# Chunked attention and a routed expert layer: tokens stored by expert together with their data, instead of lists and row gathers

## The chip, the core and the metric

The kernel runs on one NeuronCore of a Trainium2 chip. A core has a matrix engine (TensorE, "PE" in the profile, with its weight loads as "PEld"), a vector engine (VectorE, "DVE"), a scalar engine (ScalarE, "ACT"), a general engine (GpSimd, "POOL"), and a queue engine (SyncE, "SP") that issues DMA transfers. ScalarE and GpSimd issue transfers too. All transfers of the core run on the same 16 DMA engines. The engines run side by side and wait for one another on semaphores.

The metric is the device time of one execution in microseconds (us), as the median of several runs.

## What is computed

Attention within chunks of 64 positions, then a router that sends each token to one of eight experts, each a two-layer network. Cut to what matters:

```python
# q, k, v: (8, 8, 576, 64) = batch, heads, positions, head size
scores = q_c @ k_c.T / sqrt(64)          # within chunks of 64 positions
attn = softmax(scores)
out = attn @ v_c
# bridge: (B, H, S, D) -> x of (4608 tokens, 512)

xn = x / (norm(x) + 1e-6)
en = expert_emb / (norm(expert_emb) + 1e-6)
logits = xn @ en.T / tau                 # 8 experts
expert_idx = argmax(logits, axis=1)
gate_w = softmax(logits)[own expert]
for e in range(8):
    mask = expert_idx == e
    h = maximum(x[mask] @ w1[e], 0)      # w1[e]: 512 x 1024
    out[mask] = gate_w[mask] * (h @ w2[e])   # w2[e]: 1024 x 512
```

All of it is in float32. Which token goes to which expert is only known when the kernel has computed the logits, so the second half works on addresses from data.

## The kernel before

The **attention stage** goes through 36 tiles of 128 tokens (`NT = 36`), as a software pipeline: in pass `t` tile `t+7` is loaded, `t+3` is transposed, scores of `t+2` and values of `t` are computed, then the logits of `t-2`. Every four tiles the router picks the experts and counts each token's place within its expert.

```python
def values(t):
    ...                                   # pv = attention weights @ v
    x = wk.tile([P, NPAIR, 2, Dh], FP32, tag="x", name="x", bufs=3)
    nc.vector.tensor_tensor(x..., pv[...], rs..., ALU.mult)
    nc.gpsimd.dma_start(out=x_rows[P * t : P * t + P, :], in_=x)
```

Each token also has a record of 16 words, `rec`: its 8 logits, the four numbers of its quarter rows (4 x token + 0..3), its own number (`TOK`) and the sum of its squares (`SQ`). A record is scattered to the token's place in the list `spots`, where every expert has room for all tokens:

```python
def put(n):
    for at, m in to_put[:n]:              # at: places of 128 tokens, m: their records
        nc.gpsimd.indirect_dma_start(out=spots, out_offset=...(ap=at, axis=0), in_=m, ...)

def clear_spots():                        # all places get a number that is no token's
    nc.sync.dma_start(out=spots..., in_=empty...)   # 2.3 MB, in pass 0
```

The **expert stage** works on groups of 64 places of one expert, two groups (`s` = 0 and 1, one for each half of the partitions) in a step `j`. For these inputs there are 73 groups, so 37 steps: 3 early ones (`NE`), whose groups are the first three of the first and of the last expert, and 34 more. 36 steps are laid out in the code; the rest are under `tc.If`. A step's tokens are read from the list, and their x gathered in four quarters of 128 columns:

```python
def load_quarters(j, eng=nc.sync, e_t=ENG.SP):
    for s in range(2):
        row = number(src_row[...], SPARE, e_t)      # a register from SBUF
        group[s, j] = spots[ds(row, G), :]
        for b in range(G // Q):                     # 2 loads of 32 x 4 numbers
            eng.dma_start(out=quarter[:, j, c : c + 1], in_=group[s, j][...])

def load_tokens(j, eng=nc.sync):                    # the records, 64 B a token
    for s in range(2):
        eng.dma_start(out=spot[G * s : G * s + G, j], in_=group.pop((s, j)))

def gather_x(j, n=N, parts=range(P // Q)):
    xin[j] = xin_sb[j % XBUF]                       # XBUF = 3
    for c in parts:                                 # 4 gathers of 128 rows of 512 B
        nc.gpsimd.indirect_dma_start(
            out=xin[j][:, c * P : c * P + P], out_offset=None,
            in_=x_rows[0:n].rearrange("n (r d) -> (n r) d", d=P),
            in_offset=...(ap=quarter[:, j, c : c + 1], axis=0), ...)
```

Then `turn_xb(j)` transposes x in blocks of 32 x 32 on VectorE, `hidden` multiplies by w1 in four parts (`h_ps`, line 247), and `result` by w2 (`y_ps`, line 267):

```python
def hidden(j, turn=None):
    for s in range(2):
        for b in range(G // Q):
            hidden_part(j, s, b, ps_h, "h")
        if s == 0 and turn is not None:
            turn_xb(turn)
            if turn + XBUF < NJ:
                gather_x(turn + XBUF)

def result(j, ps_y):
    ...                                             # matmuls, y scaled by the gate
    nc.gpsimd.indirect_dma_start(out=out, out_offset=...(spot[:, j, TOK]), in_=y, ...)
```

In the steady part TensorE does `hidden(j+1)`, then `result(j)`, and so on. `gates(j)` computes the gate from the record on VectorE and ScalarE. The weights of the next groups (2 MB for each of w1 and w2 and each half) are loaded by SP into the second buffers, where the expert changes.

The **seam** is between the two: the last tiles' places, the table of groups (`groups`, `places`) and the first lists, while TensorE works on the three early steps. Their tokens are found early, from the first 20 tiles:

```python
    if t == early_t - 2: count_early()              # early_t = 27
    if t == early_t:     load_early()               # the records of the early groups
    ...                                             # quarter numbers by a small matmul
    if t > early_t + 3:  gather_x(i // 4, PLACED, [i % 4])   # one or two in a pass
    ...
groups(); places(0, 2); gather_x(2, PLACED); turn_xb(1); hidden_part(0, 1, 1, ps_t, "tr")
places(2, NST)
...
load_spot(NE); gather_x(NE); load_spot(NE + 1); gather_x(NE + 1); ...
```

The start loads, in this order: the experts' vectors, q and k of tiles 0 and 1, v of batch 0, q and k of tiles 2 and 3, v of batch 1. q goes through GpSimd, k and v through SP.

Of the kernel before, what the change touches and what calls it, by code (L numbers as in the profile page):

```python
# [18 lines left out]
P = 128  # L19
# [6 lines left out]
def kernel(  # L26
# [41 lines left out]
    x_rows = nc.dram_tensor("x_rows", (N, D), FP32, kind="Internal").ap()  # L68

# [3 lines left out]
    TOK, SQ = E + 4, E + 5  # L73
    SPARE = E * N
    FOLD = SPARE // P + 1
    spots = nc.dram_tensor("spots", (P * FOLD, MW), FP32, kind="Internal").ap()

# [11 lines left out]
    quarter = keep.tile([P, NJ, P // Q], I32, name="quarter")  # L89
# [38 lines left out]
    group = {}  # L128

    def load_quarters(j, eng=nc.sync, e_t=ENG.SP):  # L130
        for s in range(2):
            row = number(src_row[G * s : G * s + 1, j - NE : j - NE + 1], SPARE, e_t)
            group[s, j] = spots[ds(row, G), :]
            for b in range(G // Q):
                c = s * (G // Q) + b
                eng.dma_start(
                    out=quarter[:, j, c : c + 1],
                    in_=group[s, j][Q * b : Q * b + Q, E : E + 4]
                    .bitcast(I32)
                    .rearrange("i r -> r i")  # L140
                    .unsqueeze(2),
                )

    def load_tokens(j, eng=nc.sync):
        for s in range(2):
            eng.dma_start(out=spot[G * s : G * s + G, j], in_=group.pop((s, j)))

    def load_spot(j):
        load_quarters(j)
        load_tokens(j)  # L150

    def gather_x(j, n=N, parts=range(P // Q)):


        xin[j] = xin_sb[j % XBUF]
        for c in parts:
            nc.gpsimd.indirect_dma_start(  # L157
                out=xin[j][:, c * P : c * P + P],
                out_offset=None,
                in_=x_rows[0:n].rearrange("n (r d) -> (n r) d", d=P),  # L160
                in_offset=bass.IndirectOffsetOnAxis(ap=quarter[:, j, c : c + 1], axis=0),
                bounds_check=n * (D // P) - 1,
                oob_is_err=False,
            )

    def load_early():

        for s in range(2):
            r0 = (0, E - 1)[s] * N
            nc.scalar.dma_start(  # L170
                out=spot[G * s : G * s + G, 0:NE],
                in_=spots[r0 : r0 + G * NE, :].rearrange("(j p) m -> p j m", p=G),
            )
# [120 lines left out]
    with (  # L294
# [20 lines left out]
        FB = 17  # L315
        empty = one.tile([P, FB, MW], FP32, name="empty")
        io_i = one.tile([P, NST], I32, name="io_i")
        io = one.tile([P, NST], FP32, name="io")
        rec = one.tile([P, NT, MW], FP32, name="rec")
# [11 lines left out]
        eqb = one.tile([P, NT, E], BF16, name="eqb")  # L331
        e_of = one.tile([P, NST], FP32, name="e_of")


        same = one.tile([P, P // Q, Q], FP32, name="same")
        in_q = one.tile([P, P // Q], FP32, name="in_q")
        no_q = one.tile([P, P // Q], FP32, name="no_q")
        q_of = one.tile([P, 1], FP32, name="q_of")
# [3 lines left out]
        tok4 = one.tile([P, NE, P // Q], FP32, name="tok4")  # L342

        def constants():
            nc.gpsimd.iota(
                rec[:, :, E : E + 4].bitcast(I32),
                pattern=[[4 * P, NT], [1, 4]],
                base=0,
                channel_multiplier=4,
            )  # L350
            nc.gpsimd.iota(
                rec[:, :, E + 4 : MW].bitcast(I32),
                pattern=[[P, NT], [0, MW - E - 4]],
                base=0,
                channel_multiplier=1,
            )
# [4 lines left out]
            nc.gpsimd.memset(empty.bitcast(I32), NO_ROW)  # L361
            nc.gpsimd.memset(ones, 1.0)
            nc.gpsimd.memset(before, 0.0)
            nc.gpsimd.memset(jump[:, 1], 1.0)
            nc.gpsimd.memset(nb[:, 0:1], float((SPARE + N) // G))
# [3 lines left out]
            nc.gpsimd.tensor_scalar(e_base, io[:, 0:E], float(N), None, ALU.mult)  # L369
            nc.gpsimd.tensor_scalar(second, at, float(G), None, ALU.is_ge)  # L370
            nc.gpsimd.tensor_scalar(step, second, -2.0, 1.0, ALU.mult, ALU.add)
# [3 lines left out]
            nc.gpsimd.tensor_tensor(ends_e, ends_e, full, ALU.add)  # L375

        def late_constants():
            blocks = ident.rearrange("p (c i) -> p c i", i=Q)
            nc.vector.tensor_reduce(in_q, blocks, axis=AX.X, op=ALU.add)
            for c in range(P // Q):  # L380
                nc.vector.tensor_reduce(
                    same[:, c], blocks.rearrange("p c i -> p i c"), axis=AX.X, op=ALU.add
                )
            nc.vector.tensor_tensor(no_q, in_q, io[:, 0 : P // Q], ALU.mult)
            nc.vector.tensor_reduce(q_of, no_q, axis=AX.X, op=ALU.add)
            for x in xin_sb:
                nc.vector.memset(x, 0.0)

        def clear_spots():
            nc.sync.dma_start(  # L390
                out=spots.rearrange("(p a b) m -> p a (b m)", p=P, b=FB),
                in_=empty.rearrange("p b m -> p (b m)")
                .unsqueeze(1)
                .to_broadcast([P, FOLD // FB, FB * MW]),
            )
# [19 lines left out]
        def load_v(b):  # L415

            t = v_sb[b % 2]
            for h in range(H):
                r0 = CH * (h % 2)
                nc.sync.dma_start(  # L420
                    out=t[r0 : r0 + CH, h // 2, :, 0:Dh],
                    in_=v[b, h].rearrange("(c k) d -> k c d", k=CH),
                )
            v_t[b] = t
# [53 lines left out]
        def values(t):  # L478
# [3 lines left out]
            for i in range(NPAIR):  # L482
# [14 lines left out]
            x = wk.tile([P, NPAIR, 2, Dh], FP32, tag="x", name="x", bufs=3)  # L497
            nc.vector.tensor_tensor(  # L498
                x.rearrange("p i r d -> p r i d"),
# [4 lines left out]
            x = x.rearrange("p i r d -> p (i r d)")  # L504
            nc.gpsimd.dma_start(out=x_rows[P * t : P * t + P, :], in_=x)  # L505
            st[t] = {"x": x}

        def turn_x(t):
            d = st[t]
            ps = ps_t.tile([P, KD, P], FP32, tag="tr", name="tr")  # L510
            for c in range(KD):
# [6 lines left out]
                junk, d["x"], AF.Square, accum_out=rec[:, t, SQ : SQ + 1]  # L518
# [13 lines left out]
        def pick(b):  # L532
# [3 lines left out]
            lg = rec[:, t : t + n, 0:E]  # L536
# [12 lines left out]
        def place(b):  # L549
# [33 lines left out]
            if t + n < NT:  # L583
                with nc.allow_low_precision("whole numbers up to 36"):
                    if n == 1:
                        nc.vector.tensor_tensor(before, before, eqb[:, t], ALU.add)
                    else:
                        nc.vector.tensor_reduce(
                            before,
                            eqb[:, 0 : t + n].rearrange("p s e -> p e s"),  # L590
                            axis=AX.X,
                            op=ALU.add,
                        )
            to_put.extend((dest[:, i : i + 1], rec[:, t + i]) for i in range(n))

        to_put = []

        def early_rows(part):


            ps = rt_ps[:, 3, 1:4].rearrange("p a b -> p (a b)")[:, 0 : NE * (P // Q)]
            ps = ps.rearrange("p (j c) -> p j c", j=NE)
            if part == 0:
                nc.vector.scalar_tensor_tensor(
                    out=tok4,
                    in0=spot[:, 0:NE, TOK : TOK + 1].bitcast(I32).to_broadcast([P, NE, P // Q]),
                    scalar=float(P // Q),
                    in1=in_q.unsqueeze(1).to_broadcast([P, NE, P // Q]),
                    op0=ALU.mult,
                    op1=ALU.mult,  # L610
                )
            elif part == 1:
                nc.tensor.matmul(
                    ps, lhsT=same.rearrange("p c i -> p (c i)"), rhs=tok4, start=True, stop=True
                )
            else:
                nc.vector.tensor_scalar(quarter[:, 0:NE], ps, q_of, None, ALU.add)

        def count_early():
# [3 lines left out]
            nc.vector.tensor_scalar(done, cnt, float(G), None, ALU.is_ge)  # L623
            for i in range(1, NE):
                nc.vector.tensor_scalar(full, cnt, float(G * (i + 1)), None, ALU.is_ge)
                nc.vector.tensor_tensor(done, done, full, ALU.add)
            nc.vector.tensor_tensor(done, done, ends_e, ALU.mult)

        def put(n):

            for at, m in to_put[:n]:
# [9 lines left out]
                tc.add_to_no_dep_group("spots", ins.ins)  # L641
            del to_put[:n]

# [5 lines left out]
        def groups():  # L649
# [21 lines left out]
                jump[:, 0], nb[:, 0:E], -float(G), float(N), ALU.mult, ALU.add  # L671
# [65 lines left out]
        nc.sync.dma_start(out=emb, in_=moe_expert_emb)  # L737
        nc.sync.dma_start(out=tau_sb, in_=moe_tau.unsqueeze(0).to_broadcast([E, 1]))
        for t in range(2):
            load_qk(t)  # L740
# [3 lines left out]
        load_v(0)  # L744
        for t in range(2, 4):
            load_qk(t)
        load_v(1)
        constants()

# [175 lines left out]
```

## Time and profile before

| | |
|---|---|
| median of 3 runs | 796.28 us (792.1 to 801.57) |
| span of the profiled run | 796.7 us |
| mean granted TensorE clock | 0.963 |
| moved by the core's DMA engines | 133.14 MB, mean 167 GB/s |
| packets, and those under 512 B | 147384, 109076 |
| GpSimd's indirect DMAs | 160 gathers of x, 37 scatters of y, 36 scatters of records |

Attention lasts until some 215 us of the span, the expert steps from then on. "Busy" of TensorE is modelled and overlaps, so its rate is read from how many records fall into a stretch, not from its busy time. In the chain of waits each line is a start, a duration and what took that time. Two weight-and-matmul records stand for one float32 matmul of the code.

### The profile page before, as it was taken

What the parts mean: (1) busy time and instruction counts of PE and PEld (TensorE: products, weight loads), DVE (VectorE), ACT (ScalarE), POOL (GpSimd) and SP (SyncE); (2) the same over time, 40 slices, a digit from 0 to 9 for tenths busy, and PEclk for the clock granted to TensorE, in tenths of its full rate; (3) what the DMA queues carried; (4) which work ended last, traced back from release to release, by engine and by line L of the source; (5) the groups of instructions that cost most, each with busy time, mean ns of one, the idle gap of its engine ahead of it and who ended that gap; (6) DMA issues with size and microseconds to landing.
All of it is one profiled execution on the core that took longest, in us unless ns stands there. A gap on an engine that the chain in (4) does not pass through costs nothing.

```text
span 796.7 us, 25216 instructions
## 1 busy us (share of the span) xinstructions
PE 719.9 (90%) x10328; PEld 504.4 (63%) x10328; DVE 269.1 (34%) x755; ACT 288.5 (36%) x518; POOL 295.9 (37%) x337
## 2 busy tenths in 40 slices
PE   2699999988668899999999999999999999999994
PEld 2588888877335566767567566666667565665651
DVE  1387777765352122222212212213212222122100
ACT  3265666544113224242332332423333333324102
POOL 5135555534553333333423433332434334234130
PEclk9999999997758999999999999999999999999998
DMA  9999999998113561114676515789651444412240
GB/s 164 228 275 235 246 238 229 228 301 316 43 25 114 188 225 36 35 36 148 218 274 207 191 34 196 255 299 341 232 172 36 141 147 147 134 36 80 83 141 10
DMA packets 147384, 133.14 MB, mean 167 GB/s; under 512 B 109076, under 2 KB 111828, under 8 KB 147264
## 3 DMA queue, kind: packets, MB, share of 16 engines
q1 hardware_dynamic: 131792, 92.99, 42.2%
q0 software_dynamic: 15056, 38.46, 16.1%
q8 instruction: 83, 1.36, 0.7%
q14 instruction: 37, 0.30, 0.1%
q10 hardware_dynamic: 416, 0.02, 0.0%
HBM read 349.63 MB, written 21.80 MB: 466 GB/s over the span
## 4 chain that ended last, share of the span: by engine, by line
PE 80%; issue 7%; DMA 4%; DVE 3%; SPq 2%; another core or an unknown queue 2%; POOL 1%; ACT 0%; POOLq 0%; DVEq 0%
PE h_ps L247 32%; PE y_ps L267 32%; PE rt_ps L524 3%; PE tr L431 3%; DMA kx<-in_k_dram 2%; PE sc L447 2%; PE pv L487 2%; PE tr L473 2%; PE tr L512 2%; SPq L420 2%; DMA w<-in_moe_w_dram 1%; DVE x L498 1%; POOL qx L408 0%; DMA qx<-in_q_dram 0%
## 5 line engine op out<-in xcount | busy, mean ns | idle before, releaser
L247 PE MATMUL h_ps<-w,xbT 128*32 128x256 f32 x4736 | 304.7, 387 | 12.2 <-issue 9.2
L267 PE MATMUL y_ps<-w,hT 128*32 128x512 f32 x2368 | 298.8, 593 | 10.9 <-issue 9.5
L247 PEld LDWEIGHTS h_ps<-w,xbT 128*32 128x32 f32 x4736 | 235.2, 111 | 72.0 <-issue 40.2
L157 POOL DMA_INDIRECT xin<-x_rows,quarter x160 | 161.3, 1008 | 184.7 <-DVE xbT L208 130.8
L267 PEld LDWEIGHTS y_ps<-w,hT 128*32 128x32 f32 x2368 | 127.4, 110 | 145.9 <-issue 133.3
L257 DVE STREAM_TRANSPOSE hT<-h 128x512 f32<-128x512 f32 x74 | 52.6, 711 | 337.7 <-ACT h L256 311.6
L256 ACT ACTIVATE h<-h_ps 128x512 f32<-128x512 f32 x74 | 44.2, 597 | 262.3 <-PE h_ps L247 202.2
L276 POOL DMA_INDIRECT out_dram<-y,spot x37 | 37.6, 1016 | 187.5 <-ACT y L275 173.9
L275 ACT ACTIVATE y<-y_ps,gate 128x512 f32<-128x512 f32 x37 | 25.4, 687 | 94.7 <-PE y_ps L267 89.9
L228 ACT ACT_TABLE_LOAD x37 | 47.5, 1283 | 24.7 <-DVE sh L227 8.8
L505 POOL DMA_DIRECT2D x_rows<-x x36 | 20.6, 573 | 78.1 <-DVE x L498 52.5
L223 ACT ACT_TABLE_LOAD x37 | 47.5, 1283 | 2.9 <-DMA w<-in_moe_w_dram 2.2
L514 ACT COPY xT<-tr 128x512 f32<-128x512 f32 x36 | 21.1, 587 | 71.8 <-PE tr L512 54.2
L524 PE MATMUL rt_ps<-enT,xT 128*128 128x8 f32 x288 | 37.2, 255 | 10.9 <-DVE rec L540 8.7
L524 PEld LDWEIGHTS rt_ps<-enT,xT 128*128 128x128 f32 x288 | 37.5, 202 | 12.9 <-DVE rec L540 4.8
L431 PE MATMUL tr<-ident,kx 128*128 128x128 f32 x144 | 24.7, 298 | 22.0 <-DMA kx<-in_k_dram 21.3
L632 POOL DMA_INDIRECT spots<-rec,dest x36 | 36.4, 1012 | 19.1 <-issue 14.0
L208 DVE STREAM_TRANSPOSE xbT<-xin 128x256 f32<-128x256 f32 x74 | 43.4, 624 | 0.1
L408 POOL DMA_DIRECT2D qx<-in_q_dram x40 | 35.2, 884 | 21.6 <-PE tr L431 20.0
L431 PEld LDWEIGHTS tr<-ident,kx 128*128 128x128 f32 x144 | 18.6, 154 | 22.9 <-issue 20.7
L436 DVE COPY qxT<-tr 128x512 f32<-128x512 f32 x36 | 24.6, 683 | 24.7 <-PE tr L431 24.5
L455 DVE TENSOR_REDUCE mx<-sc 128x8 f32<-128x512 f32 x36 | 24.8, 690 | 21.0 <-PE sc L447 9.3
(132 smaller groups left out, 506.9 us busy)
## 6 DMA issues: line engine op xcount, KB each, us to landing
w<-in_moe_w_dram SPq DMA_DIRECT2D x146, 2048.0 KB
v<-in_v_dram SPq DMA_DIRECT2D x64, 144.0 KB
x_rows<-x POOLq DMA_DIRECT2D x36, 256.0 KB
qx<-in_q_dram POOLq DMA_DIRECT2D x32, 256.0 KB
kx<-in_k_dram SPq DMA_DIRECT2D x32, 256.0 KB
w<-in_moe_w_dram ACTq DMA_DIRECT2D x2, 2048.0 KB
xin<-x_rows,quarter POOLq DMA_INDIRECT x160
quarter<-spots SPq DMA_DIRECT2D x160, 0.5 KB
```

The source lines that it names most:

```text
L157: nc.gpsimd.indirect_dma_start(out=xin[j][:, c * P : c * P + P], out_offset=None, in_=x_rows[0:n].rearrange("n (r d) -> (n r) d", d=P), in ...
L208: nc.vector.transpose(xT[:, :, cols].rearrange("p c (b i) -> p b c i", i=Q), t[:, s * (D // 2) : (s + 1) * (D // 2)].rearrange("p (b i c) ...
L223: nc.scalar.activation(rn, spot[:, j, SQ : SQ + 1], AF.Sqrt)
L228: nc.scalar.activation(sh, sh, AF.Exp, accum_out=gate)
L247: nc.tensor.matmul(ps[Q * r : Q * r + Q, b].rearrange("p (k i) -> p k i", i=Q), lhsT=d["xT"][:, c, t0 : t0 + Q], rhs=w[:, c, r], start=(c ...
L256: nc.scalar.activation(h, ps, AF.Relu)
L257: nc.vector.transpose(hT[:, :, G * s : G * s + G].rearrange("p k (b i) -> p b k i", i=Q), h.rearrange("p b (k i) -> p b k i", i=Q),)
L267: nc.tensor.matmul(ps[Q * r : Q * r + Q], lhsT=d["hT"][:, c, Q * r : Q * r + Q], rhs=w2_sb[r // 2][buf_of(j)][:, c], start=(c == 0), stop= ...
L276: ins = nc.gpsimd.indirect_dma_start(out=out, out_offset=bass.IndirectOffsetOnAxis(ap=spot[:, j, TOK : TOK + 1].bitcast(I32), axis=0), in_ ...
L431: nc.tensor.transpose(ps[:, i], a[:, i * P : i * P + P], ident)
L524: nc.tensor.matmul(rt_ps[:, batch_of[t][0] % 2, batch_of[t][1]], lhsT=d["xT"][:, c], rhs=enT[:, c], start=(c == 0), stop=(c == KD - 1),)
L632: ins = nc.gpsimd.indirect_dma_start(out=spots, out_offset=bass.IndirectOffsetOnAxis(ap=at, axis=0), in_=m, in_offset=None, bounds_check=S ...
```

## The change

Each token's x and its record are now one row of 528 words (2112 B), built in SBUF in a ring of eight tiles (`xr`), and each tile is scattered as a whole to its tokens' places. There is no x in token order, no list of quarter numbers, and no gather: the rows of a group lie one after another, so SP loads them as blocks, at an address that it takes from a register. The places behind an expert's last token, up to a full group, are now filled by four scatters of blank rows (`pad_places`), and only the early groups' places are cleared beforehand, instead of the whole list. Early groups that are not full at the early count are padded by moving later places up. The loads at the start are in another order. It is meant to take GpSimd's row gathers, the lists and the waits between them out of the kernel.

The diff, cut to its core ("..." marks cuts):

```diff
-    x_rows = nc.dram_tensor("x_rows", (N, D), FP32, kind="Internal").ap()
...
+    W = D + MW
+    R = N + G * NE
+    spots = nc.dram_tensor("spots", (SPARE + G, W), FP32, kind="Internal").ap()
...
-    def load_quarters(j, eng=nc.sync, e_t=ENG.SP):
+    def load_rows(j, rows):
+        xin[j] = xin_sb[j % XBUF]
+        for s in range(2):
             for b in range(G // Q):
                 c = s * (G // Q) + b
+                nc.sync.dma_start(
+                    out=xin[j][:, c * P : c * P + P],
+                    in_=rows[s][Q * b : Q * b + Q, 0:D].rearrange("i (r d) -> r i d", d=P))
+            nc.sync.dma_start(out=spot[G * s : G * s + G, j], in_=rows[s][:, D:W])
...
+    def load_x(j):
+        for s in range(2):
+            row = number(src_row[G * s : G * s + 1, j - NE : j - NE + 1], SPARE, ENG.SP)
+            rows.append(spots[ds(row, G), :])
+        load_rows(j, rows)
...
-    def gather_x(j, n=N, parts=range(P // Q)):
...
+        NX = 2 * RB
+        xr = one.tile([P, NX, W], FP32, name="xr")
+        blank = one.tile([P, W], FP32, name="blank")
...
-        def clear_spots():
+        def clear_first():            # only the first NE groups of two experts, and a spare one
...
-            x = wk.tile([P, NPAIR, 2, Dh], FP32, tag="x", name="x", bufs=3)
+            x = xr[:, t % NX, 0:D]
...
-            nc.gpsimd.dma_start(out=x_rows[P * t : P * t + P, :], in_=x)
+            nc.gpsimd.iota(xr[:, t % NX, D + TOK : D + TOK + 1].bitcast(I32), ..., base=P * t, ...)
...
-            to_put.extend((dest[:, i : i + 1], rec[:, t + i]) for i in range(n))
+            to_put.extend((dest[:, i : i + 1], xr[:, (t + i) % NX]) for i in range(n))
...
+        def load_early(j):
+            early_ins.extend(load_rows(j, [first_rows(s, j, 1) for s in range(2)]))
...
+        def pad_places():
+            ...                       # 9 small VectorE operations
+            to_put.extend((pad[:, m : m + 1], blank) for m in range(H2))    # H2 = 4
...
-        for t in range(2):
+        for t in range(4):
             load_qk(t)
...
-        load_v(0)
-        for t in range(2, 4):
-            load_qk(t)
-        load_v(1)
+        load_v(0, 0, 4)
+        load_v(0, 4, NCB)             # load_v(1) and clear_first() follow in pass -1
...
-            if t > early_t + 3:
-                n = 1 if early_t + 4 < t < NT - 2 else 2
-                for i in to_gather[:n]:
-                    gather_x(i // 4, PLACED, [i % 4])
...
+            if early_t <= t < early_t + NE:      # early_t = 26
+                load_early(t - early_t)
+            put(1 if t < NT - 2 else 2)
...
         groups()
+        pad_places()
+        put(E // 2)
         places(0, 2)
-        gather_x(2, PLACED)
         turn_xb(1)
...
-    load_spot(NE)
-    gather_x(NE)
-    load_spot(NE + 1)
-    gather_x(NE + 1)
-    load_quarters(NE + 2)
+    load_x(NE)
+    load_x(NE + 1)
     load_w1(LONE)
-    load_tokens(NE + 2)
...
                     turn_xb(turn)
                     if turn + XBUF < NJ:
-                        gather_x(turn + XBUF)
+                        load_x(turn + XBUF)
```

## The prediction, written before the change was run

> **What bounds the kernel now.** I read the page first (shares, clock row, chain), then the chain piece by piece, then one-microsecond windows of TensorE beside GpSimd's timeline.
>
> ```profile
> PE 719.9 (90%) x10328; PEld 504.4 (63%) x10328; DVE 269.1 (34%) x755; ACT 288.5 (36%) x518; POOL 295.9 (37%) x337
> PEclk9999999997758999999999999999999999999998
> PE 80%; issue 7%; DMA 4%; DVE 3%; SPq 2%; another core or an unknown queue 2%; POOL 1%; ACT 0%; POOLq 0%; DVEq 0%
> L157 POOL DMA_INDIRECT xin<-x_rows,quarter x160 | 161.3, 1008 | 184.7 <-DVE xbT L208 130.8
> ```
>
> TensorE is the bound, but its busy time is modelled, so 90% doesn't mean 90% of its rate. The clock row sags at the seam between attention and experts; 7% of the chain is "issue" and 2% an unknown wait. Those are what a change can win. GpSimd's 160 gathers look harmless as a share (it is idle most of the time).
>
> The expert steps: a result part y of step j has 64 records, a hidden part h has 128. The chain of a steady step, and then the chain near the end, where three y parts follow one another and no gather runs:
>
> ```profile
> 438.06 4.86 PE y_ps L267 x40
> 442.92 0.14 issue
> 443.06 2.18 PE y_ps L267 x17
> 445.24 0.22 PE h_ps L247
> 445.46 0.21 PE y_ps L267
> 445.68 6.45 PE h_ps L247 x116
> ```
> ```profile
> 745.98 13.75 PE y_ps L267 x126
> ```
>
> Undisturbed, a y record costs 13.75/126 = 109 ns, an h record 6.45/116 = 55.6 ns, so a step 64 x 0.109 + 128 x 0.0556 = 14.1 us. From the y that starts at 321.85 us to the one at 731.61 us there are 28 steps, 14.63 us each: **0.53 us of every step is lost**, always late in y, here at its fortieth record. Four gathers of the next x ran back to back from 436.86 to 441.80, and the hole begins as the last one ends. An early step whose gathers fall into h shows it better: the timeline of GpSimd, then windows of TensorE (us, busy and records, clock, DMA share, GB/s):
>
> ```profile
> 295.84 1.02 POOL L157 DMA_INDIRECT xin<-x_rows,quarter  x1 [3.68 <-DVE xbT L208]
> 299.78 1.00 POOL L157 DMA_INDIRECT xin<-x_rows,quarter  x1 [0.30 <-issue]
> ```
> ```profile
> 297.00:298.00 1.00, 1.00 (x22) 1.00 0.24 66
> 298.00:299.00 1.00, 0.87 (x12) 1.00 0.12 45
> 299.00:300.00 1.00, 0.92 (x7) 1.00 0.06 21
> 300.00:301.00 1.00, 0.64 (x3) 1.00 0.27 66
> 301.00:302.00 1.00, 0.38 (x1) 1.00 0.42 66
> 302.00:303.00 1.00, 0.96 (x20) 1.00 0.00 0
> ```
>
> Records per us fall from 22 to 1 at full clock with the DMA engines nearly empty, and recover about 1 us after the last gather. The bursts that start at 256, 270, 281, 437, 452, 466, 481, 496, 510 and 525 us each have such a hole, 0.4 to 3 us long. Weight loads at 400 GB/s, SP's loads of row lists, and the gates' table loads each occur elsewhere without one. A single scatter of y makes none. So I read it as: **a run of indirect DMAs on GpSimd holds TensorE back**; by what means, the profile doesn't show. The seam fits: the chain waits on nothing known while GpSimd runs scatters and gathers from 195.7 to 200.7 and from 203.9 to 214.7, and there is a third hole at 235 to 241 while it gathers from 228.2 to 239.9.
>
> ```profile
> 197.25 4.21 another core or an unknown queue
> 205.15 8.26 another core or an unknown queue
> ```
> ```profile
> 230.00:235.00 5.00, 4.31 (x39) 0.50 0.24 54
> 235.00:240.00 5.00, 2.45 (x9) 0.50 0.18 42
> ```
>
> At the start the chain has a different owner: kx of the third tile is issued behind eight loads of v, and lands at 23 us. The first x is written at 32.12 us.
>
> ```profile
> 15.08 8.01 DMA kx<-in_k_dram
> 27.42 7.33 DMA kx<-in_k_dram
> ```
>
> [...]
>
> **The change part by part.**
>
> *Gathers out of the steady steps.* The 30 steps from about 307 to 746 us lose 0.53 us each: 30 x 0.53 = 16 us. The first steps lose more: holes at 259 to 263 us (about 3), 275 and 287 (0.4 and 0.5), 298 to 302 (3 us): 7 us. In the last, conditional step h crawls from 769.7 to 774.9 beside four gathers (768.9 to 773.9): about 4 us. The hole at 235 to 241 is 5 us. Sum 32 us on TensorE's own path, nothing beside it. In their place SP issues six hardware loads for each group, some 40 us ahead of their use (three x buffers, 14 us per step)[...]. I take 80% of it: **-26 us**.
>
> *The seam.* Before, two gathers for each scatter stand in GpSimd's queue, plus a write of x. After, a pass has an iota and one or two scatters, so the runs that end at 200.7 and 214.7 break up. The chain shows 4.2 + 8.3 us there; I take half, -6 us. Against it: pad_places puts 9 small VectorE operations at 0.15 to 0.2 us (as its neighbours on 128x8) ahead of the turn of step 1, which TensorE already waits for: 9 x 0.2 = +2 us. The four scatters of padding are a new run, 4 x 1.3 us: +1 to 3 us. Net **-2 us**.
>
> *Attention.* The DMA share is 1.0 to 1.26 from 5 us to 165 us at some 230 GB/s, so this stage is as much DMA as TensorE (a pass takes 4.09 us undisturbed; x of tile 5 is written at 58.82 us and of tile 28 at 163.85, 23 passes of 4.57). What counts is bytes ahead of a pass. Ahead of x of tile 28 stand q and k of 32 tiles (32 x 0.524 = 16.8 MB) and eight batches of v (9.4 MB) either way. Before, 28 writes of x (7.3 MB) and the clearing of the list (2.3 MB); after, 22 scatters, as each follows six passes later (22 x 0.27 = 5.9 MB), and 0.95 MB of clearing. That is 35.8 against 33.1 MB; 2.7 MB at 230 GB/s is 12 us. With all four q and k first and v of four chunks behind them the first x needs 2.1 + 0.5 MB, which at the start's 190 GB/s is about 17 us instead of 32, so TensorE can use that. But half of the 2.7 MB is only put off into the stage of the weight loads (8.4 MB at 390 GB/s, from 166 us), and the x of a tile now may not overwrite its place until the scatter of eight tiles before has landed, which is issued two passes before (some 6 us of slack, where three x buffers gave 12). I take 12 us, less 4 for these: **-8 us**.
>
> *Beside other work, no gain:* GpSimd's 161 us of gathers as such, SP's 160 list loads, the VectorE constants (3 us early).
>
> Sum: 796.3 - 26 - 2 - 8 = **760 us**.
>
> **The rivals.** (A) *The holes are not of the gathers* but of x's transfer itself, or of TensorE's own instruction stream. For: TensorE waits for nothing that is named, and x still moves in 512 B pieces. Against: the three y parts at the end are free of them, weight loads make none. Then only attention gains, and the time is about 785 us. (B) *The scatter becomes the bound*: 270 KB a tile through GpSimd's queue with six us of slack; when it lands late, VectorE waits to write x, GpSimd's iota waits in order ahead of the next load of q, and the loop slows. For: the DMA engines are full there. Against: in before x's write met no such wait (VectorE idle ahead of x: 1.0 us in total). Two us for each of 28 passes would cost 56 and use up the gain: 790 to 815 us. (C) *SP becomes the queue that blocks*: the early loads wait for scatters ahead of k and of the weights[...]. With k four passes ahead I give this 2 to 5 us. (D) *All holes go[...]*: 32 + 8 + 13 us: 743 us or less.
>
> **Range and chances.** D sets the lower end, A with a small cost from B or C the upper: 738 to 785 us. Faster by over 2% means under 780.4: the gather reading alone nearly gives that (796 - 26 = 770), attention alone does not. I hold the gather reading at 80%, B at 10%: faster 0.77, within 2% 0.15, slower 0.08.
>
> **What would show it.** Right: steps 14.1 us apart, with no drop of records late in y; y at 109 ns a record; the indirect DMAs down from 233 to 77; the first x scattered from a tile written at 15 to 20 us; the weight loads issued near 155 us. Wrong: steps still 14.6 us apart (A); VectorE or GpSimd waiting for a scatter ahead of x or iota (B); TensorE waiting for w or xbT (C). A seam as long as before would cost me the middle term only.

## The result and the profile after

The changed kernel takes **735.22 us** (median of 4, 730.33 to 736.52) against 796.0 us (792.1 to 801.57) in the same comparison: ratio 0.922, 95% interval 0.9151 to 0.929. I had predicted 760 us with a range of 738 to 785. The direction is right, the size is below the range. The experiments then show something that matters more than the size: most of these 61 us are not the change's.

First the profile after, from its page. The shares, the clock row, the h group and the new loads of x:

```profile
PE 687.0 (94%) x10326; PEld 422.4 (58%) x10326; DVE 267.4 (36%) x749; ACT 286.9 (39%) x518; POOL 123.8 (17%) x188
PEclk9899999998799999999999999998999999999998
...
L227 PE MATMUL h_ps<-w,xbT 128*32 128x256 f32 x4736 | 277.2, 386 | 7.7 <-DMA w<-in_moe_w_dram 4.2
...
xin<-spots SPq DMA_DIRECT2D x160, 64.0 KB
```

GpSimd's busy time fell by 172 us as the gathers went (337 operations to 188), and TensorE's by 33. The chain of this run ends in the last store and can't be followed further back, so stages are compared by landmarks instead. The windows that held the clearest hole before, now (us, PE busy and records, clock, DMA share, GB/s):

```profile
298.00:299.00 1.00, 1.00 (x16) 1.00 0.26 72
299.00:300.00 1.00, 1.00 (x16) 1.00 0.19 47
300.00:301.00 1.00, 1.00 (x12) 1.00 0.06 16
301.00:302.00 1.00, 1.00 (x16) 1.00 0.00 0
```

12 to 16 records in a window, with TensorE busy throughout, is what an undisturbed y shows (the hole before lay in h, which now shows 24 to 28); nothing falls to 1. The timeline of TensorE across one step, h and then y:

```profile
439.65 7.12 PE L227 MATMUL h_ps<-w,xbT 128*32 128x256 f32 x128
446.55 7.08 PE L247 MATMUL y_ps<-w,hT 128*32 128x512 f32 x64
453.42 1.94 PE L227 MATMUL h_ps<-w,xbT 128*32 128x256 f32 x32
```

From start to start a step is 6.90 + 6.87 = 13.77 us, where the kernel before had 14.63 to 14.74. There are also waits for weights, which the trace of before did not show. This one starts a step that takes 20.66 us; y runs at 9.55 us for 58 records afterwards:

```profile
501.65 1.05 PE L247 MATMUL y_ps<-w,hT 128*32 128x512 f32 x4
505.66 9.55 PE L247 MATMUL y_ps<-w,hT 128*32 128x512 f32 x58 [2.96 <-DMA w<-in_moe_w_dram]
```

At the start, TensorE's waits for k in the first 40 us fell from 21.3 us in four to 10.8 in two:

```profile
PE tr L400 <- DMA kx<-in_k_dram: 10.8, 2, 6.8
```

### The profile page after: what moved, and what is told of

Its sections match the earlier page's. It is cut to its first block, busy times and chain, and to the rows that moved or that the text cites. A ratio compares the mean times of both kernels' runs of the same rounds, so it can differ in the third digit from the quotient of the medians.

```text
span 733.2 us, 24795 instructions
## 1 busy us (share of the span) xinstructions
PE 687.0 (94%) x10326; PEld 422.4 (58%) x10326; DVE 267.4 (36%) x749; ACT 286.9 (39%) x518; POOL 123.8 (17%) x188
## 5 line engine op out<-in xcount | busy, mean ns | idle before, releaser
L227 PE MATMUL h_ps<-w,xbT 128*32 128x256 f32 x4736 | 277.2, 386 | 7.7 <-DMA w<-in_moe_w_dram 4.2
L247 PE MATMUL y_ps<-w,hT 128*32 128x512 f32 x2368 | 271.9, 598 | 4.0 <-DMA w<-in_moe_w_dram 3.0
L227 PEld LDWEIGHTS h_ps<-w,xbT 128*32 128x32 f32 x4736 | 185.3, 112 | 101.4 <-issue 28.7
L247 PEld LDWEIGHTS y_ps<-w,hT 128*32 128x32 f32 x2368 | 94.2, 111 | 155.3 <-issue 143.0
L590 POOL DMA_INDIRECT spots<-xr,dest x36 | 37.1, 1031 | 50.1 <-DVE rs L465 16.1
L456 PE MATMUL pv<-v,aT 64*64 64x65 f32 x1152 | 27.6, 233 | 1.5 <-issue 1.5
L456 PEld LDWEIGHTS pv<-v,aT 64*64 64x64 f32 x1152 | 22.1, 142 | 8.4 <-issue 8.2
L209 DVE TENSOR_SCALAR gate<-gate 128x1 f32<-128x1 f32 x37 | 5.7, 154 | 57.9 <-ACT sh L208 57.9
```

Of the source, the lines that this page charges most:

```text
L227: nc.tensor.matmul(ps[Q * r : Q * r + Q, b].rearrange("p (k i) -> p k i", i=Q), lhsT=d["xT"][:, c, t0 : t0 + Q], rhs=w[:, c, r], start=(c ...
L247: nc.tensor.matmul(ps[Q * r : Q * r + Q], lhsT=d["hT"][:, c, Q * r : Q * r + Q], rhs=w2_sb[r // 2][buf_of(j)][:, c], start=(c == 0), stop= ...
L456: nc.tensor.matmul(pv[CH * c : CH * c + CH, par, i], lhsT=d["aT"][r0 : r0 + CH, i, CH * c : CH * c + CH], rhs=v_t[b][r0 : r0 + CH, i, cb, ...
L590: ins = nc.gpsimd.indirect_dma_start(out=spots, out_offset=bass.IndirectOffsetOnAxis(ap=at, axis=0), in_=m, in_offset=None, bounds_check=S ...
```

## The experiments

In all of them, a step is the distance between the starts of two of ScalarE's operations y<-y_ps, and "the changed kernel" and "the kernel before" are the ones of the prediction. Each timed run stands beside runs of the kernel before on the same chip. When e1 to e4 came back, I took their reference of 736.06 us to be the changed kernel; e9 shows that it is the kernel before.

### e1 and e2: plain loads in place of the gathers

Both keep the kernel before with its lists, records and scatters and replace each gather by a plain load of the first 128 rows, so x then holds other tokens.

```diff
-            nc.gpsimd.indirect_dma_start(
-                out=xin[j][:, c * P : c * P + P], ... quarter[:, j, c : c + 1] ...
+            nc.sync.dma_start(      # e1; nc.gpsimd.dma_start in e2
+                out=xin[j][:, c * P : c * P + P], in_=x_rows[0:P, c * P : c * P + P]
             )
```

> The kernel before with every gather of x replaced by a plain load of the same 64 KB by SP from fixed rows (it leaves out the choice of tokens; lists, records, scatters and their order stay). Theory G (a run of gathers on GpSimd holds TensorE back): steady steps 13.8 us instead of 14.6, the holes of the first steps and of the seam gone, about 745 us. Rival X (the moving of x in 512 B pieces does it, whoever issues it): steps stay at 14.6 us and the time at about 796. Rival L (the lists and waits did it): the same as X, since the lists stay.

> As the run with SP, but the plain loads of fixed rows are issued by GpSimd. If the hold comes from indirect DMAs: steps of 13.8 us, about 745 us. [...]

Measured: e1 772.16 us, e2 737.53 us. Steps are 13.77 us in both, so the holes are absent without indirect gathers, whether SP or GpSimd issues the plain loads. That looked like a proof of my reading. e1 is slow for another reason: lists, tokens and x all stand in SP's queue ahead of the weights, TensorE waits 25.8 us for weights (14.2 for y's, 11.6 for h's), and single steps take 18 to 23 us.

### e3 and e4: gathers that nobody needs, in the changed kernel

```diff
                         load_x(turn + XBUF)
+                    idle(turn)   # e3: four gathers of 128 x 512 B from q into a scratch tile
+                                 # e4: by step: none, gathers, scatters, plain loads, one 2 KB gather, spaced gathers
```

> The changed kernel with four gathers of 128 rows of 512 B added in each of 32 steps, at the place where before had them, into a tile that nobody reads. Theory G: steps of 14.6 us again, 32 x 0.86 = 27 us more, about 762 us. If the gain is not of the gathers: 735 us.

> The changed kernel with idle GpSimd work that differs from step to step (step number modulo 6): none; 4 gathers of 128 x 512 B; 4 scatters of 128 x 512 B; 4 plain loads of 128 x 512 B; 1 gather of 128 x 2048 B; 4 gathers with four small memsets between. Step times read off the trace. Theory G as I hold it (any run of indirect DMAs): none 13.8, gathers 14.6, scatters 14.6, plain loads 13.8, one wide gather 14.0, spaced gathers 14.0 us. If only reading by index matters: scatters 13.8. If the bytes matter: one wide gather 14.6 and plain loads 14.6.

Measured: e3 739.77 us, e4 730.4 us (one execution). TensorE's y parts follow one another at 13.77 us in both, whatever GpSimd does beside, but for one step of 22 us that waits for weights. In e4 two of ScalarE's y come late (18.66 and 19.96 us after the one before) and the next follows sooner (8.88 and 8.31); TensorE is not held by it. 128 gathers of 1012 ns each, in bursts of four as before, leave no hole. The theory that a run of indirect DMAs as such holds TensorE back falls here. The added gathers are not free: e3 is some 10 us above the changed kernel of e10 on that chip (ratios to the kernel before 1.0027 and 0.9896). Of the 9.2 us between the two profiled executions, 3.2 lie between the x of tiles 28 and 35 and 4.9 behind the last y, not in the steps.

### e5 to e8: the real gather, one property at a time

```diff
# e5, e6: the list          # e7: the source               # e8: the destination
-ap=quarter[:, j, c:c+1]    -in_=x_rows[0:n] ...           -out=xin[j][:, c*P : c*P+P]
+ap=idx[:, c : c + 1]       +in_=qrow[0 : n * (D // P)]    +out=scr[:, c*P : c*P+P]
# idx = 4p + c in e5,                                      # and ahead of each group a
# 80p + c in e6                                            # small memset of scr on VectorE
```

> The kernel before; its gathers stay indirect DMAs from x_rows into xin, but their index is a fixed column (rows 4p + c of x_rows, so the same 128 tokens each time) in place of the loaded list; wrong tokens, everything else as before. Steady steps were 14.63-14.74 us in the kernel before, and 13.77 with plain loads from GpSimd in place of the gathers. If an indirect DMA as such costs TensorE (into xin, with a consumer), steps stay at 14.6 and the time near 795 us. If the cost comes of the listed, scattered addresses or of waiting for the lists, steps fall to 13.77 and the time to about 740.

> As the fixed-index run, but with the rows 20 tokens (40 KB) apart instead of adjacent, so the 128 pieces come from all over the first 5 MB of x_rows. If scattered DRAM addresses matter, this one has 14.6 us steps where the adjacent rows have 13.77. If only the loaded list matters, both have 13.77 us; if the indirect DMA as such does, both have 14.6.

> The kernel before with the real lists, gathering from the input q in place of x_rows (wrong numbers, same pieces and addresses). If the source tensor matters (a tensor written by this kernel, lying beside the weights or the program), steps fall to 13.77 us; if the list or the gather itself does, they stay at 14.6 us.

> The kernel before with the real gathers from x_rows by the real lists, but into a scratch tile that nobody reads (a small VectorE memset of it stands ahead of each group, so that they start at the same time); x stays zero. If the cost comes of what waits for the gathers (VectorE's transposes, and TensorE through them) or of writing xin, steps fall to 13.77 us; if the traffic or the issue itself holds TensorE, they stay at 14.6 us.

Measured: 738.13, 738.54, 736.4 and 755.04 us; **13.77 us steps in all four**. e7 is the telling one: in the compiled program every engine's instructions and waits are those of the kernel before, and only the tensor that the gathers read from differs. Its y at ScalarE, 13.78 and 13.77 us apart, with the four gathers between them as ever:

```profile
432.22 0.69 ACT L276 ACTIVATE y<-y_ps,gate 128x512 f32<-128x512 f32 x1 [2.29 <-PE y_ps L268]
446.00 0.69 ACT L276 ACTIVATE y<-y_ps,gate 128x512 f32<-128x512 f32 x1 [2.29 <-PE y_ps L268]
459.77 0.69 ACT L276 ACTIVATE y<-y_ps,gate 128x512 f32<-128x512 f32 x1 [2.30 <-PE y_ps L268]
```

If each of four different changes removes the cost, perhaps none of them did. That left the kernel before itself to be doubted. (e8 is 19 us later than e9 at the fourth y, which is of my memset: VectorE waits for gathers into the scratch tile, 14.7 us ahead of attention's rs alone.)

### e9 and e10: both kernels once more, unchanged

> The kernel before, word for word, once more. It was 796 us with steps of 14.63-14.74 us; four variants of it that keep an indirect gather in each place but alter its list, its source or its destination all had 13.77 us steps, although the one that gathers from q has the very same instructions and waits on every engine. If the long steps belong to the program (where x_rows lies, what the gathers wait for), this run has 14.63-14.74 us steps and about 796 us again. If they belong to the chip or the time at which it was measured, this run has 13.77 us steps and about 736 us, and the change is worth next to nothing here.

> The changed kernel, word for word, on the same chip as the kernel before and in the same rounds. If the difference is the program's, 735 us against 796; if it was the chip's, both near 735, with both at 13.77 us steps, and what is left of the difference lies ahead of step 3.

Measured on one chip in the same rounds: the kernel before takes **736.36 us** (20 executions), the changed kernel 729.69 (4); the reference runs of the kernel before there have 737.49, and the ratio of the changed kernel to them is **0.9896, 95% interval 0.9849 to 0.9943**. The page of the kernel before, run again:

```profile
PE 682.5 (93%) x10328; PEld 403.4 (55%) x10328; DVE 269.8 (37%) x755; ACT 285.7 (39%) x518; POOL 295.3 (40%) x337
...
PE 73%; DMA 13%; SPq 4%; DVE 4%; issue 3%; ACT 1%; POOL 0%; DVEq 0%; POOLq 0%; ACTq 0%
```

The same program, GpSimd as busy as before (295.3 us), but TensorE 37 us less busy, "issue" in the chain 3% in place of 7%, and no unknown wait. One of its steps, GpSimd and then TensorE:

```profile
435.85 1.02 POOL L157 DMA_INDIRECT xin<-x_rows,quarter  x1 [3.68 <-DVE xbT L208]
...
439.79 1.00 POOL L157 DMA_INDIRECT xin<-x_rows,quarter  x1 [0.30 <-issue]
```
```profile
436.88 6.61 PE L267 MATMUL y_ps<-w,hT 128*32 128x512 f32 x58
...
443.36 6.82 PE L247 MATMUL h_ps<-w,xbT 128*32 128x256 f32 x118
```

Four gathers (the first and the last shown) start beside y, as in the trace that I had read, and y runs through. Over all experiments, 151 reference executions of the kernel before, on four chips, took 729.7 to 741.41 us; none was near 796.

### e11 and e12: the start order alone

```diff
# e11: into the kernel before (e12: the reverse, out of the changed kernel)
-        nc.sync.dma_start(out=emb, ...); nc.sync.dma_start(out=tau_sb, ...)
-        for t in range(2): load_qk(t)
+        nc.scalar.dma_start(out=emb, ...); nc.scalar.dma_start(out=tau_sb, ...)
+        for t in range(4): load_qk(t)
-        load_v(0)
-        for t in range(2, 4): load_qk(t)
-        load_v(1)
+        load_v(0, 0, 4); load_v(0, 4, NCB)      # and load_v(1) at t == -1
```

> The kernel before with only the changed kernel's order of loads at the start: the experts' embedding and tau on ScalarE's queue, q and k of four tiles first, then v of four chunks, the rest of v, and v of the second batch two passes later. Gathers, lists and records stay. If the gain left on this chip is that of the start (8 of the 14.6 us that the changed kernel is ahead at step 3), the first x is written near 20 us in place of 30.6, that of tile 28 near 148 us in place of 156, and the time is about 8 us under the kernel before. If scattering x with its record is what brings it, the time stays at 736-737 us.

> The changed kernel with the old order of loads at the start (two tiles of q and k, all of v of one batch, two more tiles, v of the second batch). If the start is worth 8 us, this is 8 us slower than the changed kernel, about 737 us, and even with the kernel before; tile 28's x is written near 156 us. If the scatter path carries the gain, it stays near 730 us.

Measured: e11 735.59 us, ratio 1.0003 (0.9977 to 1.003): nothing. e12 733.17, ratio 0.9974 (0.995 to 0.9999), 3 to 6 us slower than the changed kernel of e10 on another chip (729.69, ratio 0.9896). In e11 the first x is written at 18.25 us, 12 us earlier, but that of tile 28 at 156.62 us, as in the kernel before (156.33). The lead is lost at the sixth x: TensorE waits for k, and the transposes that took 0.63 us take 1.06:

```profile
43.91 0.63 PE L512 MATMUL tr<-ident,x 128*128 128x128 f32 x4 [0.49 <-ACT aT L475]
...
49.02 1.09 PE L431 MATMUL tr<-ident,kx 128*128 128x128 f32 x4 [3.27 <-DMA kx<-in_k_dram]
49.90 1.06 PE L431 MATMUL tr<-ident,qx 128*128 128x128 f32 x4
```

SP had issued the clearing of the whole list (2.3 MB) at 33.55 us, ahead of that k. The changed kernel clears 0.95 MB there, and from 30 us on its longest wait is 1.8 us (e10). This suggests that the start order pays only with the smaller clearing; no run alters the clearing alone. e12 shows the other side: with the old start, but with the small clearing and without VectorE's constants, tile 28's x is written at 150.35 us, 6 us ahead of the kernel before (e9).

### e13 to e15: what the changed kernel leaves on the table

```diff
# e13: load_x by GpSimd
-            row = number(src_row[...], SPARE, ENG.SP)
+            row = number(src_row[...], SPARE, ENG.Pool)     # and nc.gpsimd.dma_start in load_rows
# e14: e13 and, at t == -3, behind load_qk(4)
+                        load_v(0, 4, NCB)                   # no longer ahead of the loop
# e15: e13 and
+        turn_xb(1)
         groups(); pad_places(); put(E // 2); places(0, 2)
-        turn_xb(1)
```

> The changed kernel, but from the fourth group on the blocks of x and the records are loaded by GpSimd with its own register, not by SP, so that SP issues only weights there. In the changed kernel one step (from y at 484.5 us) takes 21.25 us in place of 13.77: TensorE waits 3.6 us for the second weights, which SP issues 2.9 us after six loads of x, and then runs at half clock. If SP's place in the queue is the cause, that step falls to 14-17 us and the time by 3 to 7 us, to about 724-727 us. If the 8 MB of weights themselves are the limit, the step stays at 21 us and the time at 730.

> As the run with x loaded by GpSimd, and the last five chunks of the first v are issued behind k of the fifth tile, on which TensorE waits 7.2 us at 20 to 27 us in the changed kernel. If that wait is SP's order, it shortens to under 3 us, the second x is written near 27 us in place of 31.6, and the time falls by another 4 us, to about 720-723 us. If the DMA engines are full there in any case, k lands no earlier and nothing is gained.

> The changed kernel with x loaded by GpSimd from the fourth group on, and the transposes of step 1's x moved ahead of the grouping and the padding on VectorE. In the changed kernel TensorE waits 5.06 us for them and then runs the next 128 records of h at half clock for a part, 9.66 us in place of 7.11. If VectorE's order is the cause, that wait falls to under 2 us, the wait and the slow clock give 3 to 7 us, and the time is 713-717 us against 719. If the last part of h of step 0 or the weights are the true end of that wait, it stays at 719 us.

Measured: e13 **719.43 us** (ratio to the kernel before 0.9763, 0.9683 to 0.9843), e14 722.73 (0.9812, 0.9734 to 0.989), e15 **716.26** (0.9742, 0.9684 to 0.9801). The long step is gone in all three. SP's timeline ahead of that step in the changed kernel (e10):

```profile
458.18 2.91 SPq L169 DMA_DIRECT2D w<-in_moe_w_dram  x4
462.36 3.67 SPq L134 DMA_DIRECT2D xin<-spots  x2
466.23 3.17 SPq L140 DMA_DIRECT2D spot<-spots  x1
469.65 1.65 SPq L134 DMA_DIRECT2D xin<-spots  x2
471.49 1.55 SPq L140 DMA_DIRECT2D spot<-spots  x1
474.62 4.39 SPq L169 DMA_DIRECT2D w<-in_moe_w_dram  x4
480.24 6.76 SPq L134 DMA_DIRECT2D xin<-spots  x2
487.20 3.95 SPq L140 DMA_DIRECT2D spot<-spots  x1
```

The weights that TensorE misses at 492 us are issued from 474.62 us, when their buffers were already free. The waits of SP's queue from 440 to 510 us say so: in e10 it waits 0.6 us of the 70 for TensorE to free a weight buffer. It waits some 7 us for VectorE, for the most part to free an x, but half of its time goes into issuing the small loads themselves: 34.5 us, the sum of its x and record loads in that stretch, a single one up to 4.3 us. In e13 it waits for nothing but TensorE, 50 us of the 70, so each load of weights leaves at the first moment it may. Of the two lists of waits, the first is e10's, the second e13's.

```profile
SPq L134 <- DVE xbT L188: 4.5, 2, 3.8
...
SPq L169 <- PE y_ps L247: 0.4, 1, 0.4
```
```profile
SPq L169 <- PE y_ps L247: 29.9, 5, 6.4
SPq L169 <- PE h_ps L227: 20.0, 10, 4.6
```

With that, TensorE in e13 has no wait at all from 280 to 700 us. e14's further step did not show: its second x is written at 28.84 us, 2.7 earlier than in e13, its fifth at 50.46 as in e13 (50.49). The wait only moved to a later k; e13 and e14 cannot be told apart. In e15 TensorE's wait for the transposes of step 1 is no longer 5.06 us (lines below); the executions of e13 (713.89 to 725.16) and e15 (710.78 to 720.5), on two chips, overlap, so the 3 us between them are likely and not shown. By their ratios both beat both kernels.

## Why the prediction was wrong, step by step

The landmarks of four profiled executions, the pair that was predicted and the two runs on one chip (us of the stretch):

| stretch | before | after | change | before, e9 | after, e10 | change | predicted |
|---|---|---|---|---|---|---|---|
| start to x of tile 28 | 162.9 | 152.9 | -10.0 | 156.3 | 148.4 | -8.0 | -8 |
| x of tile 28 to x of tile 35 | 45.1 | 31.7 | -13.4 | 35.0 | 28.0 | -7.0 | seam: -2 |
| x of tile 35 to first y | 50.2 | 36.5 | -13.7 | 34.1 | 37.0 | +2.9 | (in the seam) |
| first y to fourth y | 56.9 | 53.6 | -3.3 | 53.3 | 50.8 | -2.5 | gathers: -26 |
| fourth y to last y | 471.3 | 449.3 | -22.0 | 446.6 | 449.9 | +3.3 | (in the gathers) |
| last y to the end | 10.4 | 9.2 | -1.2 | 10.1 | 9.2 | -0.9 | |
| sum | 796.7 | 733.2 | -63.5 | 735.4 | 723.2 | -12.2 | -36 |

The last pair are single executions; by medians the changed kernel is 7.8 us ahead there (737.49 to 729.69), so its rows carry a few us of scatter.

**"Gathers out of the steady steps", -26 us: the step that failed.** "A run of indirect DMAs on GpSimd holds TensorE back" does not hold for this program. The same gathers in the same places make no hole in e9, nor do added ones in e3. On one chip the stretch from first to last y changed by +0.8 us (-2.5 and +3.3) where I had -26. The trace that I had read held a counterexample: these four gathers (the first and the last shown) ran beside y without a hole, and that step is 13.81 us at ScalarE.

```profile
351.29 1.02 POOL L157 DMA_INDIRECT xin<-x_rows,quarter  x1 [4.86 <-DVE xbT L208]
...
355.23 1.00 POOL L157 DMA_INDIRECT xin<-x_rows,quarter  x1 [0.30 <-issue]
```
```profile
351.05 6.74 PE L267 MATMUL y_ps<-w,hT 128*32 128x512 f32 x60
```

In the pair the term looks right, -3.3 and -22.0 us, but by luck: its parts were off. I took the undisturbed step as 14.1 us from the chain's pieces, by dividing a piece's time by its records. But pieces of h and y interleave, some records stand in a neighbouring piece, and the true step is 13.77 (6.90 + 6.87). The last y's of before would have told it: they were already 6.87 us apart. So the kernel before lost 0.86 us a step, not 0.53: 30 x 0.86 = 26 us where I had 16. Against that stand the changed kernel's step of 20.66 us, 6.9 us too long, and the hole at 235 to 241 us, which I had counted here and which lies in the seam's rows.

What took the pair's number out of my range is **"the seam"**: -13.4 and -13.7, so -27.1 us, where I had -2. I had read 12.5 us of unknown waits there and taken half of them. On one chip the seam gives -4.1, so most of those 27 us did not come back with the program either.

The coincidence of gathers and holes in time was real, and was a property of the first measurements of the kernel before, not of its program. What those 792 to 801 us had in addition, some 61 us against e9, I could not bring back and can't explain; the cause of most of the pair's difference stays open. In the pair, the changed kernel's profiled execution is also 10 us slower than e10's, all of it ahead of the fourth y (the medians are 5.5 us apart), so whatever it was may have touched both, and touched the kernel with more GpSimd transfers more; that is argued, not shown. No run here could test whether gathers matter under that condition.

**"Attention", -8 us: right in size (-8.0 on one chip), wrong in its reason.** I divided 2.7 MB by 230 GB/s and called the stage as much DMA as TensorE. In the same-chip traces the whole lead is there at tile 5 (57.82 to 50.07 us), and from there to tile 28 both kernels need 98.5 and 98.3 us, 4.28 us a pass. So the bytes that differ there did not count; that TensorE sets these passes is likely and not shown. The first x came at 19.85 us instead of 30.59 (I had expected about 17 instead of 32). The last x of that stretch, in e9 and in e10:

```profile
156.33 0.69 DVE L498 TENSOR_TENSOR x<-pv,rs 128x512 f32<-128x512 f32 x1
```
```profile
148.36 0.69 DVE L467 TENSOR_TENSOR xr<-pv,rs 128x512 f32<-128x512 f32 x1
```

And "the VectorE constants (3 us early)", which I had put under no gain, lay on the path: in e9 they hold VectorE from 44.42 to 47.7 us, and the third and fourth x are 6.2 us apart where a pass is 4.1.

```profile
44.61 1.21 DVE L381 TENSOR_REDUCE same<-ident 128x32 f32<-128x128 f32 x4
...
46.14 1.57 DVE L387 MEMSET xin<- 128x512 f32 x3
```

**"The seam", -2 us: on one chip -4.1, as -7.0 and +2.9.** The gain that shows in the traces is not of broken-up runs on GpSimd. In e9 TensorE waits ahead of the small matmul for the early groups' quarter numbers, which the change removes, and then runs at a lower clock, 0.79 on average from 165 to 180 us; in e10 that is 1.00. (The clock in this window varies from run to run: 0.84 in e12, which has no such matmul, so part of the 7.0 us may be scatter.) The wait in e9, then the same window in e9 and in e10 (us, busy times of PE, PEld, DVE, ACT and POOL, clock, DMA share, GB/s):

```profile
163.14 0.39 PE L613 MATMUL rt_ps<-tok,same 128*128 128x12 f32 x2 [1.99 <-DVE tok L604]
```
```profile
165.00:180.00 15.00, 15.00 (x283) 13.73 (x287) 9.68 (x23) 7.78 (x17) 6.30 (x7) 0.79 1.03 396
```
```profile
165.00:180.00 15.00, 13.97 (x284) 10.66 (x282) 10.75 (x34) 8.61 (x20) 5.23 (x7) 1.00 1.02 386
```

The loss begins with what I had put at +2 us. The nine VectorE operations of pad_places run from 191.62 to 193.28 us in e10, 1.7 us by the trace, ahead of the transposes of step 1. I had missed what follows: with the grouping and the places that stand there too, the wait becomes 5.06 us (1.58 in e9), and h then takes 9.66 us for 128 records in place of 7.11. In the changed kernel of the pair the same h takes 8.53 us behind a wait of 3.56, at a granted clock of 0.60 from 204 to 206 us and 0.55 from 206 to 208; from 208 us on it is 1.00. First e10, then e15 with the transposes moved ahead, where h runs on:

```profile
189.03 1.93 PE L227 MATMUL h_ps<-w,xbT 128*32 128x256 f32 x32
196.03 9.66 PE L227 MATMUL h_ps<-w,xbT 128*32 128x256 f32 x128 [5.06 <-DVE xbT L188]
```
```profile
190.30 10.39 PE L227 MATMUL h_ps<-w,xbT 128*32 128x256 f32 x160
200.52 7.04 PE L247 MATMUL y_ps<-w,hT 128*32 128x512 f32 x64
```

**The rivals.** (C), SP as the queue that blocks, came true at the size I gave it: the fourth to the last y take 3.3 us longer, and e13 takes that away. But it isn't the early loads; it is what stands in SP's queue ahead of the weights. The first weight loads were not issued near 155 us either, but in the pair at 166.29 us (before: 166.19), on one chip at 162.39 us (before: 160.20), with the early loads ahead of them. (B) did not happen as a bound: iota waited for scatters 14.4 us in nine places in the changed kernel, while tiles 5 to 28 took no longer than before (98.3 us in e10, where that wait is 15.7 us). (A) was closest to the truth about the program: the holes are not of the gathers, and mainly attention gains. (D), whose 13 us were the whole of the seam's unknown waits, describes the number of the pair, with holes that the kernel before did not show again.

## What to carry to other kernels

A reading of holes in one trace is a reading of one measurement: before a change is built on it, look for the step that has the suspect and no hole, run the same program again, elsewhere, and compare the length of a steady step. Small loads that are slow to issue or wait for a buffer should not share a queue with large loads on which TensorE depends; giving x to GpSimd and leaving SP to the weights brought about as much again here (ratio to the kernel before 0.9763, on another chip) as the change itself on one chip (0.9896). And stages should be measured from landmark to landmark, not by the time per record of a piece in which two kinds are interleaved.

## What the hardware showed that I had not expected

Some waits of TensorE were charged twice, by their length and by a lower granted clock behind them, and the length alone did not tell which. In the kernel before (e9), the same weights cost two waits of 1.23 and 2.50 us. The y behind the first takes 6.63 us for 58 records, where 6.61 is undisturbed; the clock about the second is 1.00; and the two steps lose 1.5 and 2.7 us. In the changed kernel (e10) one wait of 3.59 us follows instead, the clock is 0.50 from 496 to 500 us, y takes 9.51 us for 58 records, and the step loses 7.5 us (us, PE busy and records, clock, DMA share, GB/s; e9, then e10):

```profile
521.00:523.00 2.00, 0.18 (x4) 1.00 0.60 173
523.00:525.00 2.00, 1.32 (x14) 1.00 0.13 34
```
```profile
492.00:494.00 2.00, 0.17 (x2) 1.00 0.93 345
494.00:496.00 2.00, 0.23 (x4) 0.70 0.38 112
496.00:498.00 2.00, 2.00 (x12) 0.50 0.42 78
498.00:500.00 2.00, 2.00 (x12) 0.50 0.98 344
```

So the two short waits were cheaper here than the one of about their sum. But no length of wait divides the cases: one of 3.51 us in e12 was followed by h at 7.11 us for 128 records, as undisturbed, while 2.96 us in the changed kernel of the pair were followed by y at 9.55 us, with a clock of 0.50 from 506 to 510 us, and the 1.99 us at e9's seam, shown above, by the 0.79. The ends of matmuls are modelled in the traces, so a wait that a view shows is not an exact idle time. The line of e12:

```profile
255.48 7.11 PE L227 MATMUL h_ps<-w,xbT 128*32 128x256 f32 x128 [3.51 <-DMA w<-in_moe_w_dram]
```

The other surprise is the first measurements themselves: a program whose executions on four chips lie between 729.7 and 741.4 us was measured at 792 to 801 us, with TensorE's granted clock at 1.00 in the steady steps (307 to 746 us) and a regular pattern of holes beside one kind of transfer.
